# Small TensorE products of an attention and mixture-of-experts kernel written as full 128x128 tiles

## The chip, the cores and the metric

The kernel runs on one core of one Trainium2 chip. The metric is the device time of one execution in microseconds. Before the change three runs gave 1882.15 us as median, 1880.99 us as the lowest and 1884.22 us as the highest. Names: PE is TensorE (PEld its weight loads), DVE is VectorE, ACT is ScalarE, POOL is GpSimd, SP issues most of the DMAs. A TensorE product has a stationary operand, which a weight load puts into the array, and a moving operand, whose columns stream through it.

## The reference

Three stages follow each other on 2304 tokens of width 512:

```
attention: 4 batches, 8 heads, 576 x 64; heads 0-3 local window of 32, heads 4-7 stride 32
x = heads side by side                                   # 2304 x 512

moe 1:  P = exp(x @ w_gate - max over all);  8 times: P /= row sums, P /= column sums, P *= N/E
        out = sum over 8 experts of P[:, e] * (relu(x @ w1[e]) @ w2[e])      # every token, every expert

moe 2:  logits = x @ w_gate; pairs (token, expert) in descending order of logit:
        a token goes to the first expert with room, 288 places per expert
        out[tokens of e] = relu(x[tokens of e] @ w1[e]) @ w2[e]
```

## The kernel before

Matrices are split into a high and a low f16 part, and a product of two of them is three f16 products. To use the range of f16, each weight matrix and each block of values is scaled by a power of two, and that needs the largest absolute value of a whole matrix. VectorE takes the maximum along each partition; the maximum over the 128 partitions goes through TensorE:

- `all_max` (lines 282 to 296) serves the early stages, eight times: four batches of v, two weight halves of expert 0, the gate weights (f32 products), and the maximum of the logits ahead of the Sinkhorn iterations. It multiplies 1 or 4 columns (128 partitions) by the identity, which lays them out as 1 or 4 rows of 128 in PSUM (L288), reduces the rows on VectorE (L291), puts the results on a small diagonal (L293), and multiplies that by ones to bring them back to all partitions (L295, L296).
- `power_max` (lines 913 to 922) serves all later weights, 31 times: a bf16 column times the identity gives one row of 128 (L917), VectorE reduces it to one element (L919), and a product of one row of ones with this element spreads it (L921). Only the exponent of the maximum is used, so bf16 does.

Stages of the program, in order: attention (woven with expert 0 of the first mixture), Sinkhorn woven with the rest of expert 0, experts 1 to 6 of the first mixture by a Strassen-like scheme (`l1s` with L980, `l2s` with L1036), expert 7 (L695, L713), and then the second mixture (`ffn`, L1547 and L1577 in 288 columns), which begins beside the end of expert 7.

During experts 1 to 6 the order of all engines is written out by the class `Sides`. It counts the time of the matmuls, gives every slot between products a budget of VectorE and ScalarE time, and runs three threads of side work in it: the next weights are fetched into a ring of seven 1024-column pieces, `maxima` takes their maxima (`scale`, which calls `power_max`), and `outs` splits them and stores or keeps them. A generator's `yield d, a, w` tells the planner the VectorE time, the ScalarE time and how long to wait. What is finished earlier in the planner's own clock frees ring pieces earlier and may change which matrix is chosen next.

The routing of the second mixture (`route`, `search`) finds, for the 18 x 128 tokens, the threshold key at which an expert becomes full. A search has three steps. In each, VectorE compares all keys with 39 or 40 candidates (L1210, two pieces), TensorE counts per expert by 18 accumulating products of an 8-column one-hot block with the comparison (`pcnt`, L1216), VectorE tests the counts (L1218), and a product with 8 rows of ones sums the 8 tests and spreads the sum (`pany`, L1222), from which VectorE forms the next base (L1225). There are 7 rounds of 2 searches of 3 steps, 42 steps in all. They stand between the matmuls of the expert products at distances counted in rows of matmuls (`T_CMP`, `T_GE`, `T_KEY`, `T_MID`); `spare` puts pieces of other VectorE work behind them.

Of the kernel before, what the change touches and what calls it, by code (L numbers as in the profile page):

```python
# [9 lines left out]
F32 = mybir.dt.float32  # L10
F16 = mybir.dt.float16
BF16 = mybir.dt.bfloat16
I32 = mybir.dt.int32
AF = mybir.ActivationFunctionType
OP = mybir.AluOpType
AX = mybir.AxisListType

B, H, S, D = 4, 8, 576, 64
N, DM, E, F = 2304, 512, 8, 1024
# [4 lines left out]
NT = N // 128  # L24
# [21 lines left out]
T_KEY = 7  # L46
T_MID = 3
# [208 lines left out]
class Kernel:  # L256
# [22 lines left out]
        tag = tag if tag in self.banks else "l1"  # L279
        return self.psum.tile([128, 512], F32, name=name, tag=tag, bufs=self.banks[tag])  # L280

    def all_max(self, cols, out, pads=(3, 2)):

        nc = self.nc
        k = cols.shape[1]
        yield from self.pad(pads[0])
        ps = self.bank("amx", "l1")
        nc.tensor.matmul(ps[:k, 0:128], cols, self.identf, start=True, stop=True)  # L288
        sm = self.asm if self.asm else self.sm
        m = sm.tile([4, 1], F32, name="amax4")[:k]  # L290
        nc.vector.tensor_reduce(m, ps[:k, 0:128], axis=AX.X, op=OP.max)  # L291
        d = sm.tile([4, 4], F32, name="adiag")[:k, :k]
        nc.vector.tensor_scalar(d, self.identf[:k, :k], m, None, op0=OP.mult)  # L293
        yield from self.pad(pads[1])
        nc.tensor.matmul(ps[:, 128:128 + k], self.onesf[:k], d, start=True, stop=True)  # L295
        nc.vector.tensor_reduce(out, ps[:, 128:128 + k], axis=AX.X, op=OP.max)  # L296

    def pow2_scale(self, pool, top, mx, name):

# [353 lines left out]
    def sinkhorn(self):  # L653
        nc, p, sm = self.nc, self.p, self.sm
        pf = p.rearrange("p c e -> p (c e)")
        mx = sm.tile([128, 1], F32, name="lmx")
        nc.vector.tensor_reduce(mx, pf, axis=AX.X, op=OP.max)
        al = sm.tile([128, 1], F32, name="lall")
        yield from self.all_max(mx, al, (0, 0))
        nc.vector.tensor_scalar(pf, pf, al, None, op0=OP.subtract)  # L660

        nc.scalar.activation(pf, pf, AF.Exp, scale=0.125)
        for _ in range(3):
            nc.vector.tensor_tensor(pf, pf, pf, op=OP.mult)
        yield
        for _ in range(8):
            rs = sm.tile([128, NT], F32, name="rs")
            nc.vector.tensor_reduce(rs, p, axis=AX.X, op=OP.add)
            nc.vector.tensor_scalar(rs, rs, 1e-9, None, op0=OP.add)
            nc.vector.reciprocal(rs, rs)  # L670
            nc.vector.tensor_tensor(p, p, rs[:, :, None].to_broadcast([128, NT, E]), op=OP.mult)
            yield
            ps = self.bank("pc")
            nc.tensor.matmul(ps[:, :NT * E], self.onesf, pf, start=True, stop=True)
            cs = sm.tile([128, E], F32, name="cs")
            nc.vector.tensor_reduce(cs, ps[:, :NT * E].rearrange("p (c e) -> p e c", e=E), axis=AX.X, op=OP.add)
            nc.vector.tensor_scalar(cs, cs, 1e-9, 1.0 / CAP, op0=OP.add, op1=OP.mult)
            nc.vector.reciprocal(cs, cs)
            nc.vector.tensor_tensor(p, p, cs[:, None, :].to_broadcast([128, NT, E]), op=OP.mult)
            yield  # L680
        nc.vector.tensor_tensor(p, p, self.isx[:, :, None].to_broadcast([128, NT, E]), op=OP.mult)
        yield
# [230 lines left out]
    def power_max(self, m):  # L913

        nc = self.nc
        ps = self.bank("amx", "l1")
        nc.tensor.matmul(ps[:1, 0:128], m.bitcast(BF16)[:, 1:2], self.identb, start=True, stop=True)  # L917
        d = self.sm.tile([1, 1], BF16, name="amax")
        nc.vector.tensor_reduce(d, ps[:1, 0:128], axis=AX.X, op=OP.max)  # L919
        yield 0.2, 0, 3.0  # L920
        nc.tensor.matmul(ps[:, 128:129], self.onesb[:1], d, start=True, stop=True)  # L921
        self.top = ps[:, 128:129]

    def fetch_part(self, item, q, dst):
        name, e, j = item
# [231 lines left out]
    def route_consts(self):  # L1157
        nc, cons = self.nc, self.rc
        it = lambda n, shape, dt=F32: (self.ac if n in ("tokf", "tokp", "trif") else cons).tile(shape, dt, name=n)
        def iota(n, shape, pattern, base=0, mult=0, dt=F32):  # L1160
            t = it(n, shape, dt)
            nc.gpsimd.iota(t, pattern=pattern, base=base, channel_multiplier=mult,
                           allow_small_or_imprecise_dtypes=True)
            return t
        self.jt = [iota(f"jt{k}", [128, w], [[s, w]], s) for k, (s, w) in enumerate(STEPS)]
        self.reve = iota("reve", [128, E], [[-1, E]], E)
        self.thr = iota("thr", [128, 3], [[96, 3]], 1)
        self.row0 = iota("row0", [128, 1], [[0, 1]], E * 128, 1)
        self.tok = it("tok", [128, NT, 2], BF16)
        tk = iota("tokf", [128, NT, 2], [[128, NT], [0, 2]])  # L1170
        nc.vector.tensor_copy(self.tok, tk)
        tp = iota("tokp", [128, NT], [[0, NT]], 0, 1)
        nc.vector.tensor_copy(self.tok[:, :, 0], tp)
        tri = it("trif", [128, 128])
        nc.gpsimd.memset(tri, 1.0)
        nc.gpsimd.affine_select(out=tri, in_=tri, pattern=[[1, 128]], base=-1, channel_multiplier=-1,
                                compare_op=OP.is_ge, fill=0.0)
        self.tri = it("tri", [128, 128], BF16)
        nc.vector.tensor_copy(self.tri, tri)
        self.onesb = it("onesb", [128, 128], BF16)  # L1180
        nc.vector.memset(self.onesb, 1.0)
        self.zero = it("zero", [128, 1])
        nc.vector.memset(self.zero, 0.0)
        self.ones18 = it("ones18", [128, NT])
        nc.vector.memset(self.ones18, 1.0)
        self.identh = it("identh", [128, 128], F16)
        nc.vector.tensor_copy(self.identh, self.identf)

        self.free = it("free", [128, NT])
        nc.vector.memset(self.free, 1.0)  # L1190
        self.rem = it("rem", [128, E])
        nc.vector.memset(self.rem, float(CAP))
        self.pen = it("pen", [128, E])
        nc.vector.memset(self.pen, 0.0)
        zh = self.ac.tile([128, 576], F16, name="zh")
        nc.vector.memset(zh, 0.0)
        w = zh.shape[1]
        for c in DIRECT:
            for o in range(0, XR, w):
                n = min(w, XR - o)  # L1200
                nc.sync.dma_start(out=self.xd[c * 128:c * 128 + 128, o:o + n], in_=zh[:, :n])

    def search(self, key, oh, remc, base, first):

        nc, rt = self.nc, self.rt
        for k, (step, w) in enumerate(STEPS):
            cmp = rt.tile([128, NT, w], BF16, name="cmp")
            for c0, c1 in ((0, 10), (10, NT)):
# [3 lines left out]
                                               op0=OP.subtract, op1=OP.is_ge)  # L1212
            yield (T_CMP if k else first) + T_SLOT * self.spare(1)
            ps = self.bank("pcnt")
            for c in range(NT):
                nc.tensor.matmul(ps[:E, :w], oh[:, c], cmp[:, c], start=c == 0, stop=c == NT - 1)  # L1216
            ge = rt.tile([E, w], BF16, name="ge")
            nc.vector.tensor_scalar(ge, ps[:E, :w], remc, float(step), op0=OP.is_ge, op1=OP.mult)  # L1218
            self.spare()
            yield T_GE  # L1220
            ps2 = self.bank("pany")
            nc.tensor.matmul(ps2[:, :w], self.onesb[:E], ge, start=True, stop=True)  # L1222
            nb = rt.tile([128, 1], F32, name="base")
            junk = rt.tile([128, w], F32, name="junk")
            nc.vector.tensor_scalar(junk, ps2[:, :w], float(step), base, op0=OP.min, op1=OP.add, accum_out=nb)  # L1225
# [3 lines left out]
    def route(self, ph):  # L1229

        nc, rt = self.nc, self.rt
        v = nc.vector
        B3 = [128, NT, E]
        m = rt.tile([128, NT], F32, name="m")
        oh = rt.tile(B3, BF16, name="oh")
        lm = rt.tile(B3, F32, name="lm")
        v.tensor_tensor(lm, self.lg, self.pen[:, None, :].to_broadcast(B3), op=OP.add)
        v.tensor_reduce(m, lm, axis=AX.X, op=OP.max)
# [12 lines left out]
        v.tensor_scalar(sg, b, 16, None, op0=OP.arith_shift_right)  # L1251
        kh = rt.tile([128, NT], F32, name="kh")
        v.scalar_tensor_tensor(kh, sg, 32769.0, self.free, op0=OP.add, op1=OP.mult)
        remc = rt.tile([E, 1], F32, name="remc")
        rj = rt.tile([E, E], F32, name="rj")
        v.scalar_tensor_tensor(rj, self.rem[:E], 1.0, self.identf[:E, :E], op0=OP.mult, op1=OP.mult, accum_out=remc)
        th = yield from self.search(kh, oh, remc, self.ones18[:, 0:1], T_KEY)
        kx = rt.tile([128, NT], F32, name="kx")
        v.tensor_scalar(kx, kh, th, 65536.0, op0=OP.subtract, op1=OP.mult)
        v.tensor_tensor(kx, kx, lo, op=OP.add)  # L1260
        tl = yield from self.search(kx, oh, remc, self.zero, T_MID)

        ge = rt.tile([128, 2, NT], F32, name="gegt")
        v.tensor_scalar(ge[:, 0], kx, tl, None, op0=OP.is_ge)
# [6 lines left out]
        ps = self.bank("pgg")  # L1271
        for k in range(2):
            nc.tensor.matmul(ps[:, k * NT * E:(k + 1) * NT * E], self.onesb, ac[:, k].rearrange("p c e -> p (c e)"),
                             start=True, stop=True)
# [315 lines left out]
    def layers(self):  # L1590
# [129 lines left out]
        self.rt, self.r0 = Arena([sx, w1s[:, 8192:], more.bitcast(F16)]), Arena([w1s[:, 0:4096], w1s[:, 4096:8192]])  # L1720
        for _ in range(2):
            nc.gpsimd.memset(self.rt.tile([128, 128, NT], BF16, name="oh1")[:, 96:], 0.0)
        self.z = self.rt.tile([128, 2, NT, E], F32, name="z", bufs=1)
        nc.vector.memset(self.z, 0.0)
        self.slot = self.rt.tile([128, 96, NT], BF16, name="slot", bufs=1)
# [101 lines left out]
```

## Time and profile before

| | |
|---|---|
| median of 3 runs | 1882.15 us |
| profiled execution | 1878.24 us, span 1876.5 us |
| mean granted TensorE clock | 0.987 |
| PE busy | 1819.3 us, 97% of the span, 12350 matmuls |
| PEld busy | 1055.3 us |
| DVE busy | 1196.3 us, 64% |
| ACT busy | 856.8 us, 46% |
| POOL busy | 474.2 us, 25% |

How to read it: matmuls are pipelined, so the busy time of one runs on after the next has started, and a busy share of 97% does not tell whether the array streams all the time. The distance from one start to the next does. A timeline row that ends in xN holds N equal instructions; its start is that of the first, its duration goes to the end of the last. A product's two numbers before its shape (128*8) are the partitions and columns of its stationary operand.

### The profile page before, as it was taken

Reading aid. Unit: us, or ns where it says so; the run is one execution under the profiler, and the core shown is the slowest. Engines: PE = TensorE matmul, PEld = TensorE weight load, DVE = VectorE, ACT = ScalarE, POOL = GpSimd, SP = SyncE. Lnnn points to the kernel's source line nnn. Section 1 sums busy time; section 2 is a strip of 40 time slices with the busy share of each in tenths; the row PEclk is TensorE's granted clock in tenths of the full one; section 3 lists DMA queues with packets and bytes.
Section 4 is the critical chain, followed back from the end, with each engine's and each line's share of the span. In section 5 each row is a group of like instructions: output and inputs, shape, how many; then the busy total and the mean of one; then the engine's idle time right before and its main releaser. Section 6 shows DMA issues by size and latency. Waiting matters only on the chain. (4 is left out here: it accounts for less than half of the span.)

```text
span 1876.5 us, 31960 instructions
## 1 busy us (share of the span) xinstructions
PE 1819.3 (97%) x12350; PEld 1055.3 (56%) x12350; DVE 1196.3 (64%) x3089; ACT 856.8 (46%) x1956; POOL 474.2 (25%) x467
## 2 busy tenths in 40 slices
PE   7989998999999999999999999999999999999997
PEld 5757765554455544554555554555445444577786
DVE  6745456678766476666666565766585788767640
ACT  6545542476657746774224511467421110234343
POOL 2121203145433443444002300324200001323241
PEclk8989999999999999999999999999999999999999
DMA  7121021255645446663330223165411002435460
GB/s 246 57 70 40 26 79 46 79 174 191 207 147 200 148 169 209 228 215 106 107 113 34 98 82 113 42 221 198 146 45 51 23 29 79 162 126 195 152 231 26
DMA packets 77421, 230.49 MB, mean 123 GB/s; under 512 B 8580, under 2 KB 13260, under 8 KB 68660
## 3 DMA queue, kind: packets, MB, share of 16 engines
q1 hardware_dynamic: 69588, 185.44, 28.5%
q0 software_dynamic: 7680, 43.01, 6.4%
q8 instruction: 97, 1.59, 0.4%
q14 instruction: 56, 0.46, 0.1%
HBM read 165.47 MB, written 62.94 MB: 122 GB/s over the span
## 5 line engine op out<-in xcount | busy, mean ns | idle before, releaser
L980 PEld LDWEIGHTS <-w1s 128*128 128x128 f16 x3024 | 293.1, 98 | 198.3 <-issue 2.0
L1036 PE MATMUL l<-w2h,hh 128*128 128x512 f16 x864 | 328.1, 380 | 0.0
L1036 PE MATMUL l<-w2l,hh 128*128 128x512 f16 x864 | 327.7, 379 | 0.0
L1036 PE MATMUL l<-w2h,hl 128*128 128x512 f16 x864 | 327.7, 379 | 0.0
L586 POOL TENSOR_TENSOR m2l<-raw,m2h 128x512 f16<-128x512 f32 x184 | 216.7, 1180 | 374.8 <-ACT raw L585 329.3
L980 PE MATMUL l<-sx,w1s 128*128 128x384 f16 x1728 | 288.5, 326 | 1.4 <-ACT vV L995 0.9
L1036 PEld LDWEIGHTS <-hh 128*128 128x128 f16 x1728 | 166.2, 98 | 196.1
L980 PE MATMUL l<-xh,w1s 128*128 128x384 f16 x864 | 221.0, 326 | 0.6 <-DVE iw L948 0.6
L938 DVE TENSOR_REDUCE wmx<-raw 128x1 f32<-128x512 f32 x240 | 152.0, 676 | 57.4 <-DMA raw<-in_moe_w_dram 57.4
L584 ACT ACTIVATE m2h<-raw,wscale 128x512 f16<-128x512 f32 x184 | 130.8, 711 | 86.3 <-DVE iw L950 27.3
L745 DVE SCALAR_TENSOR_TENSOR acc<-l,pe,acc 128x512 f32<-128x512 f32 x126 | 94.2, 748 | 118.6 <-PE l L1036 103.8
L892 POOL TENSOR_TENSOR raw<-raw 128x256 f32<-128x256 f32 x96 | 89.8, 939 | 307.5 <-DVE w1s L582 300.4
L698 ACT ACTIVATE hh<-l 128x256 f16<-128x256 f32 (+1 forms) x112 | 49.7, 447 | 225.9 <-PE l L695 225.8
L995 ACT ACTIVATE vV<-l 128x384 f32<-128x384 f32 x144 | 68.0, 485 | 172.0 <-PE l L980 170.0
L1036 PEld LDWEIGHTS <-hl 128*128 128x128 f16 x864 | 84.4, 98 | 102.1
L980 PE MATMUL l<-xl,w1s 128*128 128x384 f16 x432 | 141.0, 326 | 0.0
L585 ACT ACTIVATE raw<-raw,wscale 128x512 f32<-128x512 f32 x184 | 132.8, 722 | 6.0
L713 PE MATMUL l<-w2h,hh 128*128 128x512 f16 x288 | 110.1, 382 | 0.0
L713 PE MATMUL l<-w2l,hh 128*128 128x512 f16 x288 | 109.7, 381 | 0.0
L713 PE MATMUL l<-w2h,hl 128*128 128x512 f16 x288 | 109.7, 381 | 0.0
L1081 DVE SCALAR_TENSOR_TENSOR junk<-acc,raw 128x512 f32<-128x512 f32 x144 | 98.9, 687 | 7.4 <-DMA raw<-gt 5.4
L581 ACT ACTIVATE w1s<-raw,wscale 128x512 f16<-128x512 f32 x96 | 57.8, 659 | 82.0 <-POOL raw L892 57.5
(369 smaller groups left out, 3111.3 us busy)
## 6 DMA issues: line engine op xcount, KB each, us to landing
raw<-in_moe_w_dram SPq DMA_DIRECT2D x120, 512.0 KB, 4.9
sx<-sd SPq DMA_DIRECT2D x15, 1536.0 KB, 7.0
wd<-m2h SPq DMA_DIRECT2D x64, 256.0 KB, 4.8
wd<-m2l SPq DMA_DIRECT2D x64, 256.0 KB, 3.0
kq<-in_qk_dram SPq DMA_DIRECT2D x16, 592.0 KB, 3.8
sd<-sx SPq DMA_DIRECT2D x3, 1536.0 KB, 5.2
acc<-in_moe_w_dram SPq DMA_DIRECT2D x2, 2048.0 KB, 12.7
vl<-in_vl_dram SPq DMA_DIRECT2D x4, 768.0 KB, 5.6
```

The costliest lines, as they stand in the source:

```text
L581: nc.scalar.activation(hi, raw, AF.Copy, scale=s)
L584: nc.scalar.activation(hi, raw, AF.Copy, scale=s)
L585: nc.scalar.activation(raw, raw, AF.Copy, scale=s)
L586: nc.gpsimd.tensor_tensor(lo, raw, hi, op=OP.subtract)
L713: nc.tensor.matmul(ps, l[:, f, js], r[:, f], start=k == 0, stop=k == 3 * FC - 1)
L745: self.last = [nc.vector.scalar_tensor_tensor(a, ps, pe[:, c:c + 1], a, op0=OP.mult, op1=OP.add).ins]
L892: nc.gpsimd.tensor_tensor(o, x, y, op=OP.subtract)
L938: nc.vector.tensor_reduce(mx[:, 2 * q + k:2 * q + k + 1], part(q)[:, k * 512:k * 512 + 512], axis=AX.X, op=OP.max, apply_absolute_value=True)
L980: self.nc.tensor.matmul(ps, self.w1s[:, fs, x, k, d], a[y][:, d], start=first and m == 0, stop=m == 5, skip_group_check=not first)
L995: copy = lambda o, i: nc.scalar.activation(o, i, AF.Copy)
L1036: nc.tensor.matmul(ps, l[:, f, js], r[:, f], start=k == 0, stop=k == 3 * FC - 1)
L1081: self.nc.vector.scalar_tensor_tensor(junk, self.acc[:, c], 1.0, self.wgb[:, e], op0=OP.mult, op1=OP.mult, accum_out=self.lg[:, c, e:e + 1])
```

## The change

The changed products give the array a stationary operand of 128 partitions and 128 columns. `all_max` first reduces its columns to one on VectorE, then multiplies this column, read 128 times with step 0, by the identity: every partition of PSUM gets the whole row of 128, and one VectorE reduction gives the maximum on all partitions. There is one product and not two; it is in bf16, except for the logits (`exact`). `power_max` does the same, its result is kept in SBUF, and its `yield 0.2, 0, 3.0` has become `yield 0, 0, 2.0`. In `search` the stationary operand is 128 columns of the one-hot array from column 8c on, and the last of these reach into padding that is zeroed once; rows 8 to 127 of the counts are then numbers that mean nothing, and `first8` (ones in its first 8 rows, zeros below) leaves them out of the sum.

```diff
-    def all_max(self, cols, out, pads=(3, 2)):
+    def all_max(self, cols, out, pads=(3, 2), exact=False):
-        k = cols.shape[1]
+        m = cols
+        if cols.shape[1] > 1:
+            m = (self.asm if self.asm else self.sm).tile([128, 1], F32, name="amax1")
+            nc.vector.tensor_reduce(m, cols, axis=AX.X, op=OP.max)
         yield from self.pad(pads[0])
-        ps = self.bank("amx", "l1")
-        nc.tensor.matmul(ps[:k, 0:128], cols, self.identf, start=True, stop=True)
-        sm = self.asm if self.asm else self.sm
-        m = sm.tile([4, 1], F32, name="amax4")[:k]
-        nc.vector.tensor_reduce(m, ps[:k, 0:128], axis=AX.X, op=OP.max)
-        d = sm.tile([4, 4], F32, name="adiag")[:k, :k]
-        nc.vector.tensor_scalar(d, self.identf[:k, :k], m, None, op0=OP.mult)
+        ps = self.bank("amx", "l1")[:, 0:128]
+        if exact:
+            nc.tensor.matmul(ps, m.to_broadcast([128, 128]), self.identf, start=True, stop=True)
+        else:
+            nc.tensor.matmul(ps, m.bitcast(BF16)[:, 1:2].to_broadcast([128, 128]), self.identb, start=True, stop=True)
         yield from self.pad(pads[1])
-        nc.tensor.matmul(ps[:, 128:128 + k], self.onesf[:k], d, start=True, stop=True)
-        nc.vector.tensor_reduce(out, ps[:, 128:128 + k], axis=AX.X, op=OP.max)
+        nc.vector.tensor_reduce(out, ps, axis=AX.X, op=OP.max)
...
     def power_max(self, m):
-        ps = self.bank("amx", "l1")
-        nc.tensor.matmul(ps[:1, 0:128], m.bitcast(BF16)[:, 1:2], self.identb, start=True, stop=True)
-        d = self.sm.tile([1, 1], BF16, name="amax")
-        nc.vector.tensor_reduce(d, ps[:1, 0:128], axis=AX.X, op=OP.max)
-        yield 0.2, 0, 3.0
-        nc.tensor.matmul(ps[:, 128:129], self.onesb[:1], d, start=True, stop=True)
-        self.top = ps[:, 128:129]
+        ps = self.bank("amx", "l1")[:, 0:128]
+        nc.tensor.matmul(ps, m.bitcast(BF16)[:, 1:2].to_broadcast([128, 128]), self.identb, start=True, stop=True)
+        yield 0, 0, 2.0
+        self.top = self.sm.tile([128, 1], F32, name="amax")
+        nc.vector.tensor_reduce(self.top, ps, axis=AX.X, op=OP.max)
...
             for c in range(NT):
-                nc.tensor.matmul(ps[:E, :w], oh[:, c], cmp[:, c], start=c == 0, stop=c == NT - 1)
-            ge = rt.tile([E, w], BF16, name="ge")
-            nc.vector.tensor_scalar(ge, ps[:E, :w], remc, float(step), op0=OP.is_ge, op1=OP.mult)
+                nc.tensor.matmul(ps[:, :w], oh[:, c * E:c * E + 128], cmp[:, c], start=c == 0, stop=c == NT - 1)
+            ge = rt.tile([128, w], BF16, name="ge")
+            nc.vector.tensor_scalar(ge, ps[:, :w], remc, float(step), op0=OP.is_ge, op1=OP.mult)
...
-            nc.tensor.matmul(ps2[:, :w], self.onesb[:E], ge, start=True, stop=True)
+            nc.tensor.matmul(ps2[:, :w], self.first8, ge, start=True, stop=True)
...
-        oh = rt.tile(B3, BF16, name="oh")
+        ohp = rt.tile([128, (NT - 1) * E + 128], BF16, name="oh")
+        oh = ohp[:, 0:NT * E].rearrange("p (c e) -> p c e", e=E)
...
+            nc.gpsimd.memset(self.rt.tile([128, (NT - 1) * E + 128], BF16, name="oh")[:, NT * E:], 0.0)
```

The planner's order moves with the yield. On PE, at the end of expert 3 and the start of expert 4, the maximum of the second weight matrix of expert 5 stands like this before (l are the PSUM tiles of the expert products, w2 and hh, hl the operands of the second layer, w1s and xh those of the first):

```order
L1036 LDWEIGHTS hh
L1036 MATMUL l_9108<-w2l,hh 128x512
L1036 LDWEIGHTS hl
L1036 MATMUL l_9108<-w2h,hl 128x512
L917 LDWEIGHTS wmx_9106
L917 MATMUL amx<-identb,wmx_9106 1x128
L980 LDWEIGHTS w1s
L980 MATMUL l_9147<-xh,w1s 128x384
```

And the same maximum in the changed kernel:

```order
L978 LDWEIGHTS w1s
L978 MATMUL l_9377<-xl,w1s 128x384
L978 LDWEIGHTS w1s
L978 MATMUL l_9377<-xh,w1s 128x384
L917 LDWEIGHTS wmx_9325
L917 MATMUL amx<-identb,wmx_9325 128x128
L978 LDWEIGHTS w1s
L978 MATMUL l_9353<-sx,w1s 128x384
```

It has moved from the boundary of the two layers to a place 108 matmuls into the first layer of expert 4.

On DVE, the maximum of the logits ahead of Sinkhorn (lmx the column, adiag the diagonal, lall the result) before:

```order
L657 TENSOR_REDUCE lmx<-p 128x1
L834 TENSOR_TENSOR sx<-sc,sx 128x768
L291 TENSOR_REDUCE amax_3270<-amx 1x1
L699 SCALAR_TENSOR_TENSOR hl<-l_3246,hh 128x256
L293 TENSOR_SCALAR adiag<-identf,amax_3270 1x1
L938 TENSOR_REDUCE wmx_3366<-raw 128x1
L296 TENSOR_REDUCE lall<-amx 128x1
L938 TENSOR_REDUCE wmx_3366<-raw 128x1
L699 SCALAR_TENSOR_TENSOR hl<-l_3281,hh 128x256
L660 TENSOR_SCALAR p<-p,lall 128x144
```

And now:

```order
L657 TENSOR_REDUCE lmx<-p 128x1
L834 TENSOR_TENSOR sx<-sc,sx 128x768
L296 TENSOR_REDUCE lall<-amx 128x1
L699 SCALAR_TENSOR_TENSOR hl<-l_3226,hh 128x256
L660 TENSOR_SCALAR p<-p,lall 128x144
```

Two reductions and the diagonal have become one reduction, and two maxima of weights stand behind the subtraction (L660) that stood ahead of it.

## Rows read from the trace of the kernel before

**Rows 1.** Stretches: busy PE, PEld, DVE, ACT, POOL (x instructions), then clock, DMA, GB/s.

```profile
334.00:1407.00 1073.00, 1065.36 (x5674) 548.64 (x5674) 706.51 (x1520) 565.07 (x1050) 309.18 (x283) 1.00 0.42 143
1555.00:1790.00 235.00, 227.11 (x2386) 158.69 (x2383) 170.03 (x738) 70.30 (x144) 67.95 (x74) 0.99 0.40 143
```

**Rows 2.** Timeline (start us, us, instruction, [idle <-releaser]) of PE, pcnt and pany.

```profile
1560.22 0.38 PE L713 MATMUL l<-w2l,hh 128*128 128x512 f16 x1
1560.43 0.38 PE L713 MATMUL l<-w2h,hl 128*128 128x512 f16 x1
1560.74 0.61 PE L1216 MATMUL pcnt<-w1s,sx 128*8 128x40 bf16 x18
1561.29 0.39 PE L713 MATMUL l<-w2h,hh 128*128 128x512 f16 x1
...
1562.38 0.38 PE L713 MATMUL l<-w2h,hl 128*128 128x512 f16 x1
1562.69 0.19 PE L1222 MATMUL pany<-w1s,onesb 8*128 8x40 bf16 x1
1562.81 0.39 PE L713 MATMUL l<-w2h,hh 128*128 128x512 f16 x1
```

**Rows 3.** Timeline of PE around the two products of one power_max.

```profile
370.21 0.38 PE L1036 MATMUL l<-w2h,hl 128*128 128x512 f16 x1
370.52 0.22 PE L917 MATMUL amx<-identb,wmx 128*1 128x128 bf16 x1
370.67 0.39 PE L1036 MATMUL l<-w2h,hh 128*128 128x512 f16 x1
...
376.94 0.38 PE L1036 MATMUL l<-w2h,hl 128*128 128x512 f16 x1
377.25 0.17 PE L921 MATMUL amx<-amax,onesb 1*128 1x1 bf16 x1
377.36 0.39 PE L1036 MATMUL l<-w2h,hh 128*128 128x512 f16 x1
```

**Rows 4.** Timeline of PE around a small product with a full stationary tile.

```profile
1662.63 0.66 PE L1547 MATMUL mm<-xg,acc 128*128 128x288 f16 x4
1663.13 0.17 PE L1323 MATMUL pp<-raw,tri 128*128 128x2 bf16 x1
1663.15 0.53 PE L1547 MATMUL mm<-xg,acc 128*128 128x288 f16 x3
```

**Rows 5.** Weight loads by form: busy us, mean ns, idle before.

```profile
L1216 PEld LDWEIGHTS <-sx 128*8 128x8 bf16 x756 | 21.4, 84 | 13.7 <-issue 10.6 <-DVE w1s L1210 1.4 <-DVE h2l L1554 0.5
L1147 PEld LDWEIGHTS <-hh 128*128 128x128 f16 x64 | 3.4, 96 | 0.2
```

**Rows 6.** Timeline of PE, runs of small products with full tiles.

```profile
1554.24 0.17 PE L1148 MATMUL pl<-lw,hl 128*128 128x8 f16 x1
...
1554.44 0.17 PE L1148 MATMUL pl<-lw,hl 128*128 128x8 f16 x1
...
1672.15 1.28 PE L1392 MATMUL pidx<-raw,sx 128*128 128x6 bf16 x18
```

**Rows 7.** Timeline of DVE, then of PE, over one search step.

```profile
1653.56 0.26 DVE L1225 TENSOR_SCALAR_CACHE_REDUCE w1s<-pany,w1s 128x39 f32<-128x39 f32 x1 [0.71 <-PE pany L1222]
...
1653.86 1.08 DVE L1210 SCALAR_TENSOR_TENSOR w1s<-w1s,jt 128x390 bf16<-128x390 f32 x2
1655.68 0.25 DVE L1218 TENSOR_SCALAR w1s<-pcnt,w1s 8x39 bf16<-8x39 f32 x1 [0.74 <-PE pcnt L1216]
...
1653.33 0.19 PE L1222 MATMUL pany<-w1s,onesb 8*128 8x39 bf16 x1
1653.45 1.64 PE L1547 MATMUL mm<-xg,acc 128*128 128x288 f16 x12
1655.03 0.62 PE L1216 MATMUL pcnt<-w1s,sx 128*8 128x39 bf16 x18
```

**Rows 8.** DVE pieces behind spare, in the second mixture: busy us, mean ns, idle before.

```profile
L1388 DVE TENSOR_TENSOR sx<-w1s,raw 128x864 bf16<-128x864 bf16 x12 | 7.0, 601 | 0.1
```

**Rows 9.** Timeline of PE at the boundary of experts 3 and 4.

```profile
873.10 0.22 PE L917 MATMUL amx<-identb,wmx 128*1 128x128 bf16 x1 [2.77 <-DVE wmx L942]
```

**Rows 10.** Timeline of PE around an early all_max (attention).

```profile
20.57 0.38 PE L288 MATMUL amx<-identf,vmx 128*4 128x128 f32 x2 [1.62 <-DVE vmx L360]
...
22.07 0.58 PE L295 MATMUL amx<-adiag,onesf 4*128 4x4 f32 x2
```

More of the change, by code (lines that the diff above doesn't have):

```diff
@@ L658, in sinkhorn @@
         al = sm.tile([128, 1], F32, name="lall")
-        yield from self.all_max(mx, al, (0, 0))
+        yield from self.all_max(mx, al, (0, 0), True)
         nc.vector.tensor_scalar(pf, pf, al, None, op0=OP.subtract)
@@ L1181, in route_consts @@
         nc.vector.memset(self.onesb, 1.0)
+        self.first8 = it("first8", [128, 128], BF16)
+        nc.vector.memset(self.first8, 0.0)
+        nc.vector.memset(self.first8[:E], 1.0)
         self.zero = it("zero", [128, 1])
@@ L1253, in route @@
         v.scalar_tensor_tensor(kh, sg, 32769.0, self.free, op0=OP.add, op1=OP.mult)
[L1254 to L1257, printed above, removed]
+        remc = rt.tile([128, 1], F32, name="remc")
+        rj = rt.tile([128, E], F32, name="rj")
+        v.scalar_tensor_tensor(rj, self.rem, 1.0, self.identf[:, :E], op0=OP.mult, op1=OP.mult, accum_out=remc)
+        th = yield from self.search(kh, ohp, remc, self.ones18[:, 0:1], T_KEY)
         kx = rt.tile([128, NT], F32, name="kx")
@@ L1260, in route @@
         v.tensor_tensor(kx, kx, lo, op=OP.add)
-        tl = yield from self.search(kx, oh, remc, self.zero, T_MID)
+        tl = yield from self.search(kx, ohp, remc, self.zero, T_MID)
         ge = rt.tile([128, 2, NT], F32, name="gegt")
```

## The prediction

> **What bounds the kernel now.** I read the stretches first. In experts 1 to 6 TensorE is busy for 1065.4 of 1073 us and in the second mixture for 227.1 of 235, at a granted clock of 1.00 and 0.99 [rows 1]; VectorE, next, has 706.5 and 170.0 us. So TensorE's order of work sets the time there, and an instruction costs what it adds between two starts. That is read from the timeline of PE, around the products that the change touches.
>
> The second look is at one `pcnt`. Matmuls of 512 columns start 0.21 to 0.22 us apart (1560.22 to 1560.43, 0.215 taken below), but the first `pcnt` starts 0.31 us after the last of them, so 0.095 is added. Its 18 products take 0.61 us in all, of which the last takes 0.18, so they start (0.61 - 0.18) / 17 = 0.025 apart; 18 of those are 0.45, yet the next large matmul starts 0.55 after the first: another 0.10 [rows 2]. The same two gaps stand around every small product with an 8- or 1-wide side: `pany` starts 0.31 after its predecessor and holds up its successor by 0.12 [rows 2], L917 starts 0.31 after its predecessor and needs 0.15 for 128 columns that stream in 0.055 (a quarter of 0.215), and L921 starts 0.31 after its own [rows 3].
>
> The third look asks whether being small, or waiting for VectorE, makes the gap. `pp` (L1323) has two columns, waits for VectorE too, and has a full 128x128 stationary tile. It starts 0.50 us after the first of four matmuls of 288 columns, so 0.125 after the last, and its successor 0.02 after it [rows 4]: no gap on either side. So I put the gap down to the shape of the stationary operand, at 0.095 us for each change from full to small and back.
>
> **The change part by part.**
>
> Search. Each of the 42 steps has one `pcnt` and one `pany`. Each loses a gap ahead (0.095) and one behind (0.095): 42 x 0.38 = 16.0 us, if the 18 wide products run as fast as the narrow ones and nothing else becomes late.
>
> The pace of the wide ones is the first unknown. Their loads bring 128 columns where they brought 8. Loads of 128 neighbouring columns, new ones for each product, run at one every 0.025 us (eight starts from 1554.24 to 1554.44) in `pl`; loads whose columns lie 18 elements apart run at (1.28 - 0.20) / 17 = 0.064 in `pidx`, the last product's 0.20 taken off [rows 6]. The new ones read neighbouring columns, but start 8 columns apart, which no row has. I take 0.025, since step 1 is what they share with `pl`; the other end costs 756 x 0.039 = 29 us. None of it can be a gain, as `pcnt` is at 0.025 already.
>
> On VectorE nothing gets dearer: 128 partitions take the time of 8 (0.26 us for L1225 on 128x39, 0.25 for L1218 on 8x39) [rows 7].
>
> What may become late is VectorE's chain. In the step shown `pany` starts at 1653.33, the comparison ends at 1653.86 + 1.08 = 1654.94, and `pcnt` starts at 1655.03, twelve matmuls later, 0.09 after its operand [rows 7]. With the gaps gone it would start 0.19 earlier, at 1654.84. Its first ten products need only the first half of the comparison and last 0.25, so the eleventh would come at 1655.09, 0.15 after the end. A free VectorE just suffices; where `spare` puts a piece of other work (L1388, 0.60 us) in between [rows 8], the wait moves to `pany` and part of the 0.38 is not won. There are 4 such pieces for most rounds, two dozen in all. If each takes its 0.3 back, 8 us stay; I take 13 of 16.0.
>
> `power_max`, 31 times. L917 loses 0.095 ahead and 0.095 behind; its 128 columns stay. L921 goes: 376.94 to 377.36 is 0.42, less the 0.215 of its predecessor, 0.205 [rows 3]. Together 0.395 x 31 = 12.2 us in a stretch that TensorE bounds. The reduction on VectorE has 128 elements per partition as before. Three or four of the products wait for VectorE or a DMA anyway and give less: 11 is the low end. The new load repeats one column 128 times, which no row shows; as it is one load and a matmul of 0.215 us runs above it, a load of 0.096 us [rows 5], or of twice that, stays hidden.
>
> `all_max`, 8 times. One bf16 product takes the place of L288 (0.38 us from first start to last end) and L295 (0.58) [rows 10], and the chain loses a pass through TensorE and two short VectorE operations. At the full 0.8 us that is 6 us; TensorE waits in these stages (1.62 us for `vmx` in the same row), and then it is nothing. I take 2.5.
>
> The planner. With 0.2 us less VectorE time and 1.0 us less waiting for each maximum, side work runs ahead of the old order, and two matrices of the second mixture are fetched earlier. One place matters: at the boundary of experts 3 and 4 TensorE stands for 2.77 us, waiting for a weight maximum [rows 9]. In the new order this product stands 108 matmuls further on, so its operand, at the same lag, is there. The other side work may find its DMA or POOL late somewhere else: from +4 us won to 8 lost; I take 2.5 won. The memsets added (first8, the pads) run where no product waits for them yet: 0.
>
> Sum: 13 + 12.2 + 2.5 + 2.5 = 30.2 us. The profiled execution took 1878.24, the span and 1.7 us around it, 3.9 under the median of 1882.15. Its own time would become 1848, and the median **1852**.
>
> **The rivals.**
>
> The wide loads do not overlap. Place: the 756 products of `pcnt`. If each load, 96 ns long at 128 columns [rows 5], is in the way of the next product, the pace is 0.096 and the cost 756 x 0.071 = 54 us: 1906, slower. The change gains nothing from a pace of 0.025 + 30.2 / 756 = 0.065 on. For it: no load has started at such an offset. Against it: `pl` hides loads of 96 ns at 0.025, and the narrow loads that are hidden now take 84 ns, hardly less [rows 5, 6]. The Trainium skill speaks against the change here (TensorE: Matmul & The Clock Gate, LDWEIGHTS (loading the stationary operand)): a load takes columns / 1.2 ns. By that figure, an estimate, 120 more columns are 100 ns more per load and 76 us in all if none is hidden; the trace does not bear the rule out, with 84 ns for 8 columns and 96 for 128.
>
> The loads run like those of `pidx`, at 0.064: 29 us dearer, 1881, no change. For it: the starts that are not multiples of 128 columns; against it: step 1.
>
> The gap belongs to the wait and not to the shape. Then only L921 goes: 31 x 0.205 = 6.4, with the 2.5 of `all_max` and 2.5 of the planner 11.4: 1871. Against it stands `pp`, which waits and has no gap [rows 4]. The Trainium skill has a rule that bears on this (TensorEngine Tiling (Array Packing), Key Properties): changing the tiling mode drains TensorE. By that rule alone this rival would fall away; it names no price, and `pp` agrees with it.
>
> The new order of the side work finds other waits, and VectorE's chain takes all it can: 8 + 11 + 0 - 5 = 14 us: 1868.
>
> **How the numbers follow.** The forecast gets 0.76; waits that take half back 0.10; the gap from the wait 0.06; loads at 0.064 0.05; loads that do not overlap 0.03. The forecast's own range is 1845 (16.0 + 12.2 + 6 + 3) to 1860 (8 + 11 + 0 + 3). To hold the time 8 times in 10 the range is **1844 to 1867**; outside lie the last three of these cases (0.14) and about half of the second. A measurement here can tell 0.2%, 3.8 us, from no change. Faster: 0.76 + 0.10 + 0.06 and 0.02 of the loads at 0.064, 0.94. Within 0.2%: 0.03 of that case. Slower: 0.03.
>
> **What would show it.** In the new profile the step from the last large matmul to `pcnt`, `pany` and the maxima is 0.215 or 0.122, and from them to the next large one the product's own time; `pcnt` takes about 0.61 us for 18 (1.3 would be the pace of `pidx`, 1.8 that of loads not hidden). L921 and L295 are gone. The stretch of experts 1 to 6 is some 14 us shorter, the second mixture some 13. Waits of PE for L1218 and L1210 grow by about 3 us in all; above 8 the search estimate is wrong. The wait of 2.77 us is gone; new ones of TensorE on L917, w1s or w2 would make the planner's term wrong.

## The result and the profile after

The changed kernel takes 1863.57 us (median of 4 runs, 1860.97 to 1865.46), the kernel before 1881.57 (median of 4, 1879.73 to 1884.22): a ratio of 0.9902, 95% interval 0.9884 to 0.9920, or 18.4 us (15.1 to 21.8). The prediction said 1852 with 1844 to 1867; its sum was 30.2 us.

First the stretches again. A stage is cut here at starts of matmuls that both kernels have: the first of expert 1, the first of the last expert, the first `pcnt`, the last `pany`, the last matmul. The columns are those of [rows 1]; first the kernel before, then the changed one.

```profile
0.00:334.10 334.10, 304.14 (x2827) 213.91 (x2828) 191.52 (x467) 164.60 (x650) 67.47 (x75) 0.94 0.23 79
334.10:1407.70 1073.60, 1065.32 (x5674) 548.61 (x5674) 707.14 (x1519) 565.06 (x1049) 309.18 (x283) 1.00 0.42 143
1560.70:1784.00 223.30, 215.41 (x2263) 150.66 (x2263) 160.34 (x683) 67.61 (x138) 66.32 (x72) 0.99 0.42 150
```

```profile
0.00:332.00 332.00, 299.57 (x2802) 212.59 (x2803) 186.03 (x459) 164.60 (x650) 66.63 (x75) 0.94 0.23 80
332.00:1396.80 1064.80, 1054.77 (x5645) 550.58 (x5645) 716.98 (x1546) 566.67 (x1049) 309.28 (x285) 1.00 0.42 144
1549.70:1766.80 217.10, 203.24 (x2264) 153.43 (x2263) 160.35 (x683) 67.53 (x138) 66.89 (x72) 0.98 0.43 154
```

The early stage is 2.1 us shorter, experts 1 to 6 are 8.8 shorter, the stage of the searches 6.2. The two stages that are not shown changed by 0.2 together. In the last pair PE's busy time falls by 12.2 us while the stage gets only 6.2 shorter: TensorE now waits there for 13.9 us (217.10 - 203.24), against 7.9 before.

The gaps themselves are gone. The PE timeline of one `power_max` and of one search step answers to [rows 3] and [rows 2]:

```profile
537.77 0.38 PE L1034 MATMUL l<-w2h,hl 128*128 128x512 f16 x1
537.98 0.22 PE L917 MATMUL amx<-identb,wmx 128*128 128x128 bf16 x1
538.04 0.38 PE L1034 MATMUL l<-w2h,hh 128*128 128x512 f16 x1
...
1560.31 0.38 PE L713 MATMUL l<-w2h,hl 128*128 128x512 f16 x1
1560.53 0.62 PE L1217 MATMUL pcnt<-w1s,sx 128*128 128x40 bf16 x18
1560.99 0.38 PE L713 MATMUL l<-w2h,hh 128*128 128x512 f16 x1
1561.21 0.38 PE L713 MATMUL l<-w2l,hh 128*128 128x512 f16 x1
1561.42 0.38 PE L713 MATMUL l<-w2h,hl 128*128 128x512 f16 x1
1561.64 0.18 PE L1223 MATMUL pany<-w1s,first 128*128 128x40 bf16 x1
1561.67 0.38 PE L713 MATMUL l<-w2h,hh 128*128 128x512 f16 x1
```

`pcnt` starts 0.22 after a product of 512 columns (it was 0.31) and takes 0.46 to the next large start (0.55); `pany` starts 0.22 after its own and holds its successor up by 0.03 (0.31 and 0.12). L917 starts 0.21 after (0.31) and costs 0.06 (0.15). L921 is gone. The 18 wide products take 0.62 us like the narrow ones: the 756 loads with 128 columns, which start 8 columns apart, run as fast as those of `pl`. Over all starts between large products, the medians give 0.18 us per `pcnt` and 0.19 per `pany`, 42 x 0.37 = 15.5 us of the 16.0 in the prediction.

What came in their place is seen in the waits. Of PE, and then of VectorE for the gathered tokens, in the stage of the searches (us in total, times, longest); first before, then changed:

```profile
PE pcnt L1216 <- DVE w1s L1210: 2.1, 3, 0.8
PE pany L1222 <- DVE w1s L1218: 1.0, 2, 0.7
DVE osc L1469 <- DMA g<-xd,raw: 4.4, 7, 1.0
```

```profile
PE pcnt L1217 <- DVE w1s L1211: 4.6, 6, 2.4
PE pany L1223 <- DVE w1s L1219: 3.3, 4, 1.6
DVE osc L1471 <- DMA g<-xd,raw: 7.9, 8, 2.9
```

`osc` is one column of VectorE work in `ffn_x`, a product of the gathered tokens' weights with a scale (`iws`). It waits for a gather, and VectorE's queue is in order, so everything behind it waits too. The longest case, on VectorE and then on PE:

```profile
1696.61 0.15 DVE L1471 TENSOR_TENSOR osc<-g,raw 96x1 f32<-96x1 f32 x1 [2.91 <-DMA g<-xd,raw]
1696.69 1.09 DVE L1211 SCALAR_TENSOR_TENSOR w1s<-w1s,zero,jt 128x400 bf16<-128x400 f32 x2
...
1697.37 0.82 PE L1217 MATMUL pcnt<-w1s,sx 128*128 128x40 bf16 x18 [2.42 <-DVE w1s L1211]
```

The comparison of the next search stands behind `osc`, and `pcnt` behind the comparison. In the kernel before the same `osc` came without a wait; in `pmax_oldy` below, which has the old search, it waited 1.26 us. Two `pany` wait in the same way, behind `osc` and the test of the counts (0.83 and 1.63 us). The gathers follow the next expert's four weight loads of 1 MB on one queue: this one landed 1.3 us after the last of them, and 18.8 us after the first was issued. In the kernel before it was 16.3 us from the same issue to the landing, so the gather came no sooner beside a faster TensorE.

In experts 1 to 6 the wait of [rows 9] is gone, and others have come; PE rows:

```profile
572.70 1.62 PE L978 MATMUL l<-sx,w1s 128*128 128x384 f16 x9 [0.70 <-ACT vV L993]
...
613.99 0.23 PE L917 MATMUL amx<-identb,wmx 128*128 128x128 bf16 x1 [0.84 <-DVE wmx L940]
...
685.42 0.23 PE L917 MATMUL amx<-identb,wmx 128*128 128x128 bf16 x1 [1.06 <-DVE wmx L940]
...
873.81 1.14 PE L978 MATMUL l<-sx,w1s 128*128 128x384 f16 x6 [1.27 <-ACT vU L993]
```

Together 3.9 us for the 2.77 that went.

### The profile page after: what moved, and what is told of

Its sections match the earlier page's. It is cut to its first block, busy times and chain, and to the rows that moved or that the text cites. A ratio compares the mean times of both kernels' runs of the same rounds, so it can differ in the third digit from the quotient of the medians.

```text
span 1859.2 us, 31850 instructions
## 1 busy us (share of the span) xinstructions
PE 1791.8 (96%) x12296; PEld 1058.9 (57%) x12296; DVE 1192.3 (64%) x3081; ACT 858.3 (46%) x1956; POOL 474.0 (25%) x469
## 5 line engine op out<-in xcount | busy, mean ns | idle before, releaser
L584 ACT ACTIVATE m2h<-raw,wscale 128x512 f16<-128x512 f32 x184 | 130.9, 712 | 63.3 <-DVE iw L948 17.1
L582 DVE SCALAR_TENSOR_TENSOR w1s<-raw,wscale,w1s 128x512 f16<-128x512 f32 x96 | 83.0, 904 | 20.2 <-ACT w1s L581 20.2
```

The costliest lines, as they stand in the source:

```text
L582: nc.vector.scalar_tensor_tensor(lo, raw, s, hi, op0=OP.mult, op1=OP.subtract)
L584: nc.scalar.activation(hi, raw, AF.Copy, scale=s)
```

## The experiments

Theory: each gap comes of the stationary operand's shape; the full tiles take all gaps away, and part of the gain comes back as waits of TensorE, in the searches because VectorE's queue holds instructions that wait for gathers, in experts 1 to 6 because the planner's new order is worse and not better. Rivals: VectorE's chain with its spare pieces is too long by itself; and the order is worth nothing, or what was predicted.

Each run is compared with the kernel before on its own chip. The chips differ: the kernel before takes 1885 us on one, like the 1882 of the prediction, and 1908 to 1913 on three others, so only ratios and differences within one chip count. The microseconds given with a ratio are worked out from it; the difference of the two medians can be up to 1.7 us less or more (9.7 in `search_only`).

**One part at a time.** `search_only` is the kernel before with the new `search` (and `first8` and the padding) alone; its core is

```diff
-                nc.tensor.matmul(ps[:E, :w], oh[:, c], cmp[:, c], start=c == 0, stop=c == NT - 1)
+                nc.tensor.matmul(ps[:, :w], oh[:, c * E:c * E + 128], cmp[:, c], start=c == 0, stop=c == NT - 1)
...
-            nc.tensor.matmul(ps2[:, :w], self.onesb[:E], ge, start=True, stop=True)
+            nc.tensor.matmul(ps2[:, :w], self.first8, ge, start=True, stop=True)
```

> The kernel before with the search's part of the change alone (pcnt and pany on full tiles, the padded one-hot tile); power_max and all_max as before. The prediction's term is 13 us, to about 1868.5. Theory of the gathers: the 42 mode-change gaps go, but some 6 us come back as waits of TensorE, since VectorE's osc multiplication waits for a gather whose landing does not move; the search stage was 6.2 us shorter in the profile of the changed kernel, so about 1875.4. Rival, the waits in the search stage come from the power_max part (it shifts the planner's order and the throttle's dips): then near 1868 to 1870.

Measured: 1899.19 against 1908.9, ratio 0.9940 (0.9923 to 0.9956), 11.4 us (8.4 to 14.7). By the stage of the searches it is 7.7 us: 235.2, where `before_osc` below, whose searches are those of before except that `osc` is on ScalarE, has 242.9 on the same chip. The expected 6 lies outside the interval of the time, and the rival's 13 inside it. The stage is nearer to the theory, but it is read from the slowest of the six executions (1903.9). The waits of PE for the search tests (`pany`) are 8.5 us in `search_only` and 3.9 in `before_osc`, so these waits grow with this part alone, without `power_max`.

`pmax_only` is the kernel before with the new `power_max` alone:

```diff
-        ps = self.bank("amx", "l1")
-        nc.tensor.matmul(ps[:1, 0:128], m.bitcast(BF16)[:, 1:2], self.identb, start=True, stop=True)
-        d = self.sm.tile([1, 1], BF16, name="amax")
...
-        yield 0.2, 0, 3.0
-        nc.tensor.matmul(ps[:, 128:129], self.onesb[:1], d, start=True, stop=True)
-        self.top = ps[:, 128:129]
+        ps = self.bank("amx", "l1")[:, 0:128]
+        nc.tensor.matmul(ps, m.bitcast(BF16)[:, 1:2].to_broadcast([128, 128]), self.identb, start=True, stop=True)
+        yield 0, 0, 2.0
```

> The kernel before with power_max alone changed (with its new yield). By the stages of the two profiles experiments 1 to 6 become 8.8 us shorter; the prediction's terms are 12.2 for the gaps and 2.5 for the planner. Theory: 8 to 11 us faster than before, and the search stage as long as before. Rival, the gaps' gain is 14.7 and other parts of the change gave some of it back: 14 us or more.

Measured: 1900.04 against 1907.72, ratio 0.9955 (0.9942 to 0.9969), 8.6 us (5.9 to 11.1), as the theory expected; the rival's 14 lies outside. With `after_again` (the changed kernel as it is) in the same group:

> The changed kernel, unaltered, on the same chip as the three that follow, since a chip of the runs so far was 1.4% slower than the one of the prediction. Theory: the ratio to the kernel before stays at 0.988 to 0.992, that is 15 to 22 us.

Measured: 1888.79, ratio 0.9902 (0.9886 to 0.9917), 18.7 us, as in the first result. So 11.4 + 8.6 = 20.0 of the parts stand against 18.7 for the whole: they add up within their intervals, which are too wide to tell what `all_max` gave.

`pmax_only` and `after_again` ran on one chip and differ by the search and `all_max`. The medians are 11.3 us apart, and the stages of the searches 9.6; first `pmax_only`, then `after_again`:

```profile
1557.70:1801.30 243.60, 222.28 (x2264) 152.75 (x2263) 160.47 (x683) 67.04 (x138) 64.90 (x72) 0.96 0.38 138
```

```profile
1553.00:1787.00 234.00, 209.89 (x2265) 154.82 (x2264) 159.14 (x683) 66.91 (x138) 64.87 (x72) 0.96 0.40 143
```

**The planner's order.** Three kernels take the old yield, with which SyncE's queue has the same transfers in the same order as the kernel before. `old_yield` and its second run `old_yield2` are the changed kernel with one line different; `pmax_oldy` is `pmax_only` with the same line.

```diff
-        yield 0, 0, 2.0
+        yield 0.2, 0, 3.0
```

> The changed kernel with the planner's yield in power_max as before (0.2, 0, 3.0), so that SyncE's queue keeps the order of before. Theory: the new waits in experts 1 to 6 (0.86 at 571.8, 1.0 at 612.8, 1.2 at 684.0, 1.43 and 0.43 at 872 us) come of the planner's other order, and the wait of 2.77 us at 873 returns with the old one; the two nearly cancel, so within 2 us of the changed kernel, 1861.5 to 1865.5. Prediction's reading (new order worth 2.5 us): 1866. Rival, every new wait comes of the order and the old wait goes by itself since the chain before it is shorter: 1858 to 1860.

> The kernel before with power_max alone changed, and with its old yield, so that the planner's order stays as before. Theory: the new order cost some 3 us (experts 1 to 6 took 1066.8 to 1067.6 us with it on these chips and 1063.2 with the old one in old_yield), so 11 to 13 us faster than before and experts 1 to 6 of 1063 to 1064 us. Prediction's reading (the new order is worth 2.5 us): 6 us faster, less than the 7.7 of pmax_only.

> The changed kernel with the old yield once more, beside ge_first on one chip. Theory (the new order costs 3 us): 20 to 23 us faster than before, experts 1 to 6 at 1063 to 1064 us. Rival (the order is worth nothing): 18 to 19 us, as after_again.

Measured: `old_yield` 1887.74, ratio 0.9891 (0.9873 to 0.9908); `old_yield2` 1860.29 against 1885.31, ratio 0.9866 (0.9846 to 0.9887), 25 us; `pmax_oldy` 1872.82, ratio 0.9940 (0.9920 to 0.9960), 11.3 us where `pmax_only` had 8.6. For `pmax_oldy` the theory's 11 to 13 us held, and the 6 of the prediction's reading lies outside the interval. For `old_yield2` the interval of the time, 21 to 29 us, reaches into the theory's 20 to 23, but its stretch of experts 1 to 6 missed it (1066.9 us for 1063 to 1064). The stretch of experts 1 to 6, first `pmax_oldy`, then `pmax_only`:

```profile
333.70:1396.80 1063.10, 1054.00 (x5645) 550.61 (x5645) 708.03 (x1519) 565.12 (x1049) 308.68 (x283) 1.00 0.42 145
```

```profile
337.70:1404.70 1067.00, 1055.07 (x5645) 550.55 (x5645) 716.87 (x1546) 566.83 (x1049) 309.00 (x283) 1.00 0.42 144
```

PE has the same 5645 matmuls; VectorE has 27 instructions and 8.8 us more with the new order, as side work moved in from later. In all profiles of kernels with the new `power_max`, six with the new order take 1064.8 to 1067.6 us here (mean 1066.6), five with the old one 1063.1 to 1066.9 (mean 1064.4). The ranges overlap because of two profiles with the old order, `old_yield2` (1066.9) and `ge_first` (1065.0). In both TensorE's granted clock stood at 1.2 GHz for 3.4 us right after the wait at the boundary of experts 3 and 4; the wait and that stretch in `old_yield2`:

```profile
868.33 0.23 PE L917 MATMUL amx<-identb,wmx 128*128 128x128 bf16 x1 [2.18 <-DVE wmx L940]
...
868.80:872.20 3.40, 3.40 (x13) 1.61 (x12) 0.13 (x1) 0.65 (x2) 0.00 (x0) 0.50 1.02 429
```

The three others with the old order take 1063.1 to 1063.9, less than each of the six with the new one. So the new order costs 2 to 3 us, where the prediction had it win 2.5. In `pmax_oldy` the wait at the boundary of experts 3 and 4 is back:

```profile
866.48 0.23 PE L917 MATMUL amx<-identb,wmx 128*128 128x128 bf16 x1 [2.70 <-DVE wmx L940]
```

So the prediction was right that this one wait belongs to the order, and wrong that the order as a whole gains. `old_yield` also has the lowest ratios of the versions that were measured twice, 0.9891 and 0.9866 against 0.9902 twice; as the chips differ and the intervals overlap, that it is faster than the changed kernel is likely and not shown.

**Shape or wait.** `pany64` cuts `pany` to 64 rows.

```diff
-            nc.tensor.matmul(ps2[:, :w], self.first8, ge, start=True, stop=True)
+            nc.tensor.matmul(ps2[:, :w], self.first8[:64], ge[:64], start=True, stop=True)
```

> The changed kernel with pany's product on 64 of the 128 rows (first8 and ge cut to 64 rows; the 64 left out are zeros in first8). If the gap comes of the shape (a row tile smaller than the array), both gaps at the 21 pany products return: from the product ahead to pany 0.22 us again in place of 0.12 behind 288 columns, and from pany to the next 0.12 in place of 0.03, 4 us in all. Rival, only the smallest tiles (8 rows) pay, or the wait for a semaphore does: 0.12 and 0.03 as in the changed kernel.

There are 42 `pany`, so the expectation should have said 8 us and not 4. PE timeline of `pany64`:

```profile
1718.93 0.29 PE L1579 MATMUL mm<-h2l,w2h 128*128 128x288 f16 x1
1719.05 0.61 PE L1217 MATMUL pcnt<-w1s,sx 128*128 128x39 bf16 x18
1719.51 0.90 PE L1549 MATMUL mm<-xg,xh 128*128 128x288 f16 x6
1720.34 0.19 PE L1223 MATMUL pany<-w1s,first 64*128 64x39 bf16 x1
1720.46 0.79 PE L1549 MATMUL mm<-xg,xh 128*128 128x288 f16 x5
```

Six products 0.122 apart from 1719.51 on put the sixth at 1720.12; `pany` starts 0.22 after it and its successor 0.12 after `pany`, both as before the change, while `pcnt`, left on full tiles, has no gap on either side. `pany` waits for the same VectorE test in both forms, so the shape makes the gap, and 64 rows pay as 8 did. Over all 42 `pany` the medians say the same: behind 512 columns 0.310 us, and 0.122 to the next start, against 0.215 and 0.028 in the changed kernel and 0.311 and 0.121 before. A single execution took 1893.44 us against 1888.79 for the changed kernel: not a measure of 8 us, but no contradiction. By the Trainium skill (TensorEngine Tiling (Array Packing), Tiling Modes and Key Properties) 64 rows are a tiling mode of their own, and a change of mode drains TensorE. The trace agrees, in that a gap stands on both sides of the 64 rows, and adds the price, about 0.095 us each way.

**Is it the gathers?** In `osc_act` (and `osc_act2`), and in `before_osc` from the kernel before, `osc` moves to ScalarE; in `osc_pool`, made from `old_yield`, to GpSimd.

```diff
-        nc.vector.tensor_tensor(osc[:, s:s + 1], gs[s][:, 2 * DM:].bitcast(F32), self.places[ph][1][:M], op=OP.mult)
+        nc.scalar.activation(osc[:, s:s + 1], gs[s][:, 2 * DM:].bitcast(F32), AF.Copy, scale=self.places[ph][1][:M])
```

In `osc_pool` the added line is

```diff
+        nc.gpsimd.tensor_tensor(osc[:, s:s + 1], gs[s][:, 2 * DM:].bitcast(F32), self.places[ph][1][:M], op=OP.mult)
```

> The changed kernel with the osc product (96 x 1, one per gather, in ffn_x) on ScalarE behind its copy of the same gather's transposes, instead of on VectorE ahead of the search's comparisons. Theory of the gathers: VectorE's waits for the gathers (7.9 us in 8 waits) go from the search's chain, and of TensorE's 7.9 us of waits for L1211 and L1219 some 5 go: 1858 to 1860. Rival, VectorE's chain with its spare pieces is simply too long for the faster TensorE: within 1 us of the changed kernel, 1862.5 to 1864.5.

> The osc product on ScalarE once more, now beside the changed kernel on one chip. Theory of the gathers: TensorE's waits for L1211 and L1219 at which an osc product stood ahead (2.58, 0.99 and 1.79 us in the profile of the changed kernel) go, 3 to 5 us faster than the changed kernel. Rival, VectorE's own chain is too long: within 1 us of it.

> The kernel before with the osc product on ScalarE. VectorE waits 4.4 us for the gathers there, and TensorE 3.1 us in all for the search's comparisons. Theory (the wait was mostly hidden before and came out only as TensorE became faster): 1 to 2 us faster than before, 1880. Rival, the wait costs both kernels alike: 4 to 5 us faster, 1877.

> As old_yield2, with the osc product on GpSimd behind the three gathers that it needs; GpSimd's queue holds nothing else until the next weight loads, some 10 us later. (In osc_act and osc_act2 the product stood on ScalarE ahead of evictions and waited 13 to 15 us for the gathers there, so the wait had only changed its queue.) Theory of the gathers: in old_yield2 TensorE's waits of 1.02 at 1701.0 (pcnt), 1.69 at 1733.1 and 1.88 at 1764.0 us (pany) stand behind osc products on VectorE; they go, and the search stage becomes 3 to 5 us shorter than the kernel with the product on VectorE on the same kind of chip: 213.5 to 215.5 against 218.4 where the kernel before takes 1885, 230 to 232 against 234.7 where it takes 1908; the ratio to the kernel before is 0.984 to 0.9855, or 0.9865 to 0.988. Rival, the three waits stay or move to the next instruction: 217.5 to 219 us, ratio as before the move (0.9866 or 0.9891).

Measured: `osc_act` 1887.27, ratio 0.9893 (0.9876 to 0.9911), where the changed kernel has 0.9902 on other chips; `osc_act2` 1893.03, ratio 0.9917 (0.9902 to 0.9931), beside `after_again` with 0.9902; `before_osc` 1909.30, ratio 1.0002 (0.9990 to 1.0013); `osc_pool` 1887.46 against 1912.78, ratio 0.9868 (0.9841 to 0.9895), its search stage 236.5 us, where `old_yield` and `after_again`, on two other such chips, have 234.7 and 234.0. The first three show none of the expected gain, and `osc_act2`, 4.2 us slower than `after_again`, does not fit its rival either; their search stages point both ways (231.6 us in `osc_act` against 234.7 in `old_yield`, 236.6 in `osc_act2` against 234.0 in `after_again`). The ratio of `osc_pool` lies in the range that the theory expected, but its interval holds the 0.9891 of `old_yield` too, and its stage is no shorter, though PE's waits for the searches are 7.7 us there and 9.6 in `old_yield`: inconclusive. The first three fail for a reason that the trace shows; ScalarE in `osc_act`:

```profile
1702.06 0.41 ACT L1587 ACTIVATE yt<-mm 128x288 f32<-128x288 f32 x1 [4.10 <-PE pany L1223]
1705.23 0.29 ACT L1471 ACTIVATE osc<-g,raw 96x1 f32<-96x1 f32 x1 [2.75 <-DMA g<-xd,raw]
1706.69 0.41 ACT L1587 ACTIVATE yt<-mm 128x288 f32<-128x288 f32 x1 [1.17 <-PE mm L1579]
...
1709.70 0.81 ACT L1470 ACTIVATE xg<-ptg 128x768 f16<-128x768 f16 x1 [1.67 <-PE pany L1223]
```

`osc` was put ahead of the copy that it was meant to follow (L1470), and ScalarE waited 14.9 us for gathers, ahead of its evictions: the wait had changed its queue. `osc_pool` is clean of this, but it ran on a chip of the 1908 to 1913 kind, and there the gathers are not the main thing that TensorE waits for. In `after_again`, on such a chip, VectorE waits only 2.3 us for them, yet PE waits 7.3 us for the tests:

```profile
PE pany L1223 <- DVE w1s L1219: 7.3, 11, 1.6
PE pcnt L1217 <- DVE w1s L1211: 2.0, 4, 0.9
DVE osc L1471 <- DMA g<-xd,raw: 2.3, 3, 1.1
```

On the chip of 1885 us the pattern of the first profile is there again. `old_yield2`, VectorE, then PE:

```profile
1733.66 0.15 DVE L1471 TENSOR_TENSOR osc<-g,raw 96x1 f32<-96x1 f32 x1 [1.71 <-DMA g<-xd,raw]
...
1734.56 0.25 DVE L1219 TENSOR_SCALAR w1s<-pcnt,sx 128x40 bf16<-128x40 f32 x1
...
1734.86 0.18 PE L1223 MATMUL pany<-w1s,first 128*128 128x40 bf16 x1 [1.53 <-DVE w1s L1219]
```

`pmax_oldy`, on the same chip with the old search, has 2.6 and 1.1 us of PE's waits, `old_yield2` 3.0 and 4.1. So on both kinds of chip PE's waits in the searches grow with the new `search`, by 2.3 us (from `pmax_only` to `after_again`) to 4.8 (the first pair). That the gathers are the cause on the faster kind is read from rows like these; no run without them was made on such a chip, and it stays open as a cause.

**The spare pieces.** `ge_first` is `old_yield` with the piece that stood between comparison and test put behind the test.

```diff
-            yield (T_CMP if k else first) + T_SLOT * self.spare(1)
+            yield T_CMP if k else first
...
+            self.spare(1)
             self.spare()
```

> As old_yield2, and in a search step the spare piece that stood between the comparison and the threshold test goes behind the test. In after_again TensorE's longest waits for L1219 (1.1 at 1628.6, 1.7 at 1663.5, 1.2 at 1697.2, 0.7 at 1733.2 and 1768.1 us) have two L1390 pieces of 0.6 us ahead of the test on VectorE. Theory (VectorE's in-order queue between pcnt and pany is what gives the gain back): those go, 3 to 5 us faster than old_yield2. Rival, the pieces only move to the next wait (pcnt for L1211), or the stalls of ScalarE and VectorE by themselves make the waits: within 1.5 us of old_yield2.

Measured: 1861.59, ratio 0.9877 (0.9858 to 0.9896), beside `old_yield2` with 0.9866; its search stage is 217.8 us against 218.4, PE's waits 3.6 and 3.4 against 3.0 and 4.1. As far as two profiles tell, the pieces only move the wait from `pany` to `pcnt`: the rival of this run. Taking pieces out of the way is worth nothing here. This was on the chip of 1885 us; the waits that suggested it are those of `after_again` on a slower one, where it was not tried, so what holds up the tests there stays open.

## Why the prediction was right, and where it was not

The mechanism held in each step that was about TensorE: the gaps belong to the shape (0.095 us each way), the wide loads are hidden at 0.025 us, L921 is gone. The rivals that put the gap on the wait, or that made loads dear, fall with the first rows of the new trace.

`power_max`, predicted 12.2: `pmax_oldy`, which has this and nothing else, gives 11.3 (7.5 to 15.1) in time and by its stretch, which has 29 of the 31 (5645 matmuls for 5674), 10.5 (1063.1, against 1073.6 in the first profile of before). The term was right.

The planner, predicted +2.5 with +4 to -8: -2 to -3. The step that failed is "I take 2.5 won". The one wait that I could see in the old trace went, as said, and four of 0.7 to 1.3 us came for it. A trace shows the waits that an order has, not those that another order will have; the middle of the range, -2, was the better value.

The search, predicted 13 of 16.0: 15.5 us of gaps went, and less was kept. The stage became 6.2 us shorter in the first pair, 7.7 in `search_only`, 7.2 from `pmax_oldy` to `old_yield2` (225.6 and 218.4) and 9.6 from `pmax_only` to `after_again`. The time of `search_only` says 11.4 (8.4 to 14.7), and this interval holds the 13. A stage is read from one execution of each kernel, and those of `search_only` and `old_yield2` were the slowest of their runs; I cannot say which is nearer. By these values "I take 13" was too high by 2 to 7 us, though the time does not exclude that it was right.

Where the first pair lost it: in the profile of the changed kernel, gaps that exceed the pace of the matmul ahead by 0.4 us and more grew from 9.1 to 14.7 us, smaller waits by an estimated 2 (worked out as what is left), and the granted clock stood at 1.2 GHz for 6.8 us in place of 3.4, 1.7 us lost (it fell at 1604.6 and 1628.5 us, each time after two or three waits of 0.6 to 1.2 us): 15.5 - 5.6 - 2 - 1.7 = 6.2. The prediction had counted only spare pieces as what VectorE would be late with. It did not look at what else stands in that queue with a wait of its own, although the old trace had it: 4.4 us of `osc` waiting for gathers. How much of the loss these make is open, as said above. PE's waits for L1218 and L1210 grew by 4.8 us, between the 3 that the prediction expected and the 8 from which it would have called its estimate wrong.

`all_max`, predicted 2.5: the early stage is 2.1 shorter in this pair of profiles. Over all profiles its length runs from 332.0 to 336.9 us with this code (nine, mean 334.0) and from 333.7 to 337.7 with the old one (five, mean 335.6), so this is no more than a sign.

The sum by stages is 2.1 + 8.8 + 6.2 + 0.2 = 17.3, against 30.2. The fourth rival, in which the new order finds other waits and VectorE's chain takes all that it can, had 14 us and 1868. The measured 1863.57 lies between it and the forecast's own range, 1845 to 1860, and inside the stated 1844 to 1867 only because that range had been widened. The rival names what happened: each of its two halves came true in part, and the forecast should have borne more of it in its middle.

## What to carry to other kernels

A small product between full ones costs more by its shape than by its columns: two changes of about 0.095 us each time, here for stationary operands of 1, 8 or 64 rows and of 1 or 8 columns. Padding with zeros or reading one column 128 times cost TensorE nothing here, since the load stayed hidden. Where TensorE is made faster next to a chain through another engine, look in that engine's queue for every instruction with a wait of its own (a DMA above all): the gathers here landed no sooner, and part of the gain can be given back there. And when a planner's numbers change with an edit, run the edit with the old numbers too; here that version had the lowest ratios.

## What the runs showed of the hardware

The gap needs no small operand of 8: 64 rows have it. 96 rows do not, as `px` shows in the changed kernel, where products of 96 and 128 rows take turns:

```profile
1600.29 0.29 PE L1487 MATMUL px<-w1s 128*128 128x288 f16 x1
1600.42 0.29 PE L1489 MATMUL px<-identh,w1s 96*128 96x96 f16 x3
1600.55 0.29 PE L1487 MATMUL px<-w1s 128*128 128x288 f16 x1
```

0.13 behind 288 columns, and three products of 96 columns in 0.13: no gap either way.

The chips on which the kernel before took 1908 to 1913 us lost most of it in two places: the changed kernel's searches took 234.0 us there against 217.1, and the part behind them 87.3 against 81.2. In the searches ScalarE stood for up to 5 us with nothing that released it ("remote"), while the weight loads ran; `old_yield`:

```profile
1728.32 0.41 ACT L1554 ACTIVATE h<-mm 128x288 f32<-128x288 f32 x1 [5.05 <-remote]
```

In `after_again` these are 12.0 us in three waits for L1554, and the first profile has none. TensorE in turn waited 3.7 us for L1554, in the first profile not at all. The clock has a part as well: in the searches of `after_again` the granted clock stood at 1.2 GHz for 17.1 us, against 6.8 in the first profile of the changed kernel, and behind them for 6.8 us against none. What makes the waits of ScalarE was not tried.
